# Unread products ahead of early TensorE steps: their number taken from a replay of all engines and of TensorE's instruction supply

## The chip, the cores and the metric

The kernel runs on one core of a Trainium2 chip. Its engines are TensorE (PE in the profile, its weight loads PEld), VectorE (DVE), ScalarE (ACT), GpSimd (POOL) and SyncE (SP), which here issues nearly all transfers. The metric is the device time of one execution in microseconds (us), lower is better.

## The reference

```python
def attention(q, k, v):                    # B=8, H=8, S=576, D=64
    q_d, k_d, v_d = (a.reshape(8, 8, 144, 4, 64).mean(axis=3) for a in (q, k, v))
    out_up = np.repeat(sm_attn(q_d, k_d, v_d), 4, axis=2)     # softmax attention on means of four
    mask = np.abs(pos[:, None] - pos[None, :]) < 4            # and a local band of width 7
    scores = np.where(mask, q @ k.T / 8, -1e9)
    return out_up + softmax(scores) @ v
def ffn(x, w_in, w_out):                   # x: 4608 x 512, w_in: 512 x 2048, w_out: 2048 x 512
    h = x @ w_in
    return (h * np.cos(h)) @ w_out
```

The attention's output, 4608 tokens by 512, is the FFN's x.

## The kernel before

The attention is cut into 32 units, one for a batch and a pair of heads. The FFN works on twelve tiles of 384 tokens and sixteen chunks of 128 of the 2048 inner columns; its products are made of two f16 halves of each operand, three matmuls for one. The weights come as 64-bit words in two halves each (`wdi`, `wdo`) and are split on ACT, DVE and POOL while the first units run.

The units of batches 0 and 1 (NEARLY = 2) are the early part. Each has four steps on TensorE: local scores in `u_s` (two mask products of 128 x 192 at L1022, then 192 small products of 32 x 32 at L1028), pooled scores in `u_s` (four of 72 x 144, L1037), transposes in `u_t` (eight of 72 x 72, L1153), and in `u_pv` the pooled PV (32 of 64 x 144, L1179) and the local PV (96 small ones of 64 x 24, L1196). Between them DVE, ACT and POOL make the softmax: for the first unit the local weights are `sml`, which DVE transposes at L1136 ahead of L1196; the pooled queries and keys of the next unit (`qkd`, L721) come from a chain on DVE. The result of L1196 is copied by ACT (L651, tile `xd`) and added by DVE (L1215). Later units run in pieces (L755 to L858). `gemm1` (L1410) is the first FFN product, `gemm2` (L1430) the second, and L1335 squares weights and inputs for a bound.

The order on all engines is written by a planner (class `Plan`). It holds every operation with a cost, a list scheduler (`run`) places them, and the kernel issues them in order of the planned start times `o.start`, each engine in that order. The planner also counts TensorE's instructions (L305 to L313): with FETCH it supposes that TensorE runs out of instructions after 448, and gets 256 more at a time; the wait is `o.stall`, which is part of `o.dur`.

The loop that issues the operations (L1608 to L1640) puts unread products ahead of PE operations that are planned to start before 300 us (`fend`). Such a product, `wide(s)`, multiplies the 128 x 128 identity `ident_b` with a 128 x 512 copy of itself (L1600) into a PSUM bank that is free for the moment, and nobody reads it. It reads no new data, so it never waits for a transfer. Two rules set their number. The first fills planned gaps: between the end of the last PE operation and the planned start it takes the planned ends of the helpers' operations in between as marks, and puts 0.8 (`fill`) times the gap over 0.22 us there; the first product behind a mark waits for that helper. The second adds products while the planned busy share of PE's recent past, `share(o, t)`, is under a bound, 0.42 (`share`) or, for some us after a stall of over 1 us, 0.72 (`again`). Both count in planned times; `cur` is where PE would stand with the products put in so far.

```python
n = int((y - x) * CFG["fill"] / 0.22)
...
while 4.0 < o.start < CFG["watch"] and share(o, max(cur, o.start)) < (CFG["again"] if cur < risk else CFG["share"]):
```

## Time and profile before

| what | us |
|---|---|
| runs of the kernel, median of 3 (lowest to highest) | 912.93 (911.85 to 913.46) |
| the profiled execution, first to last instruction | 910.3 |
| TensorE busy, matmuls | 889.4 |
| DVE busy | 711.2 |
| ACT busy | 693.1 |
| POOL busy | 486.2 |
| chain that ended last, part of L1600 (unread products) | 3% |

The profile is of another execution than the three runs; its span stands 2.6 us below their median. An engine's busy time adds up its instructions; an unread product counts like any other. "issue" in a list of waits is time in which the engine waited for nothing that the profile shows. [...] In windows the columns "busy (x)" hold us and the number of instructions.

### The profile page before, as it was taken

To read this page: it belongs to the slowest core of one execution; us is meant where nothing else is said; L and a number is where in the kernel's file an instruction comes from. 1 tells how busy PE (TensorE), PEld (TensorE's weight loads), DVE (VectorE), ACT (ScalarE), POOL (GpSimd) and SP (SyncE) were. 2 spreads that over 40 slices of the span, in tenths; PEclk is the share of its full clock that TensorE was granted. 3 is DMA by queue.
4 is the path that set the end of the run, shared out by engine and by line. 5 is a ranking of instruction groups with operands and counts; after the bars stand their busy time and mean duration, and the time that the engine had idled before them with its cause. 6 is when DMAs were issued, how large, how long until landed. Compare 5 with 4: busy or idle time off the path is not lost.

```text
span 910.3 us, 28740 instructions
## 1 busy us (share of the span) xinstructions
PE 889.4 (98%) x11673; PEld 579.9 (64%) x11673; DVE 711.2 (78%) x1514; ACT 693.1 (76%) x1542; POOL 486.2 (53%) x601
## 2 busy tenths in 40 slices
PE   8999999999999999999999999999999999999996
PEld 4665665555555555677767677666776777777773
DVE  6479788888889998877689887986689867846772
ACT  3458898888678876886887886986888987776764
POOL 4288753537768875644356543653468734522221
PEclk9899999999999999999999999999999999999998
DMA  7864176205453743232433443344344431124501
GB/s 245 255 223 142 37 276 214 83 1 95 113 131 80 169 99 99 63 94 67 119 88 101 121 114 96 89 111 125 102 135 119 112 105 38 56 96 140 174 2 39
DMA packets 100863, 103.96 MB, mean 114 GB/s; under 512 B 47280, under 2 KB 73648, under 8 KB 100720
## 3 DMA queue, kind: packets, MB, share of 16 engines
q1 hardware_dynamic: 99424, 99.67, 37.5%
q0 software_dynamic: 1296, 2.36, 1.8%
q8 instruction: 93, 1.52, 0.7%
q14 instruction: 50, 0.41, 0.1%
HBM read 81.05 MB, written 16.22 MB: 107 GB/s over the span
## 4 chain that ended last, share of the span: by engine, by line
PE 83%; DVE 7%; ACT 5%; DMA 2%; issue 2%; POOL 1%; SPq 0%; DVEq 0%; POOLq 0%; ACTq 0%
PE bank L1430 36%; PE bank L1335 22%; PE bank L1410 11%; PE bank L1600 3%; PE bank L906 2%; PE bank L1203 1%; PE bank L1184 1%; PE bank L912 1%; DMA q<-qT 1%; PE bank L1179 1%; DVE prob L932 1%; PE bank L1196 1%; PE bank L858 1%; ACT L946 1%; ACT L1389 1%
## 5 line engine op out<-in xcount | busy, mean ns | idle before, releaser
L1335 PEld LDWEIGHTS <-wdi 128*128 128x128 f16 x2400 | 203.8, 98 | 59.7 <-issue 3.8
L1430 PE MATMUL bank<-wdo,gh 128*128 128x512 f16 x696 | 207.1, 379 | 0.0
L1335 PE MATMUL bank<-wdo,wdi 128*128 128x192 f16 x1344 | 141.7, 246 | 0.8 <-DVE wdi L1356 0.3
L1430 PE MATMUL bank<-wdo,gl 128*128 128x512 f16 x348 | 131.7, 379 | 0.0
L1410 PEld LDWEIGHTS <-wdi 128*128 128x128 f16 x768 | 74.3, 98 | 56.3 <-issue 2.4
L530 POOL TENSOR_TENSOR gl<-tr,gh 128x384 f16<-128x384 f32 x60 | 59.2, 987 | 69.3 <-ACT gh L1393 51.0
L1430 PEld LDWEIGHTS <-gh 128*128 128x128 f16 x696 | 63.9, 98 | 41.4 <-issue 1.5
L1430 PE MATMUL bank<-wdo,wdi 128*128 128x512 f16 x342 | 86.9, 379 | 0.5 <-ACT ob L1448 0.5
L1430 PE MATMUL bank<-wdo,wdo 128*128 128x512 f16 x315 | 79.8, 379 | 0.7 <-ACT ob L1448 0.7
L1389 ACT ACTIVATE tr<-tr 128x384 f32<-128x384 f32 x98 | 50.9, 521 | 20.8 <-DVE tr L1387 20.3
L1430 PEld LDWEIGHTS <-gl 128*128 128x128 f16 x348 | 34.0, 98 | 41.1
L1386 ACT ACTIVATE tr<-bank,bmagic 128x384 f32<-128x384 f32 x66 | 37.8, 573 | 19.0 <-PE bank L1410 9.9
L1390 ACT ACTIVATE tr<-tr 128x384 f32<-128x384 f32 x98 | 50.4, 517 | 1.2
L1391 DVE SCALAR_TENSOR_TENSOR tr<-tr,bank 128x384 f32<-128x384 f32 x66 | 36.0, 545 | 18.0 <-ACT tr L1390 17.7
L1430 PEld LDWEIGHTS <-wdo 128*128 128x128 f16 x342 | 32.1, 98 | 28.1 <-issue 1.7
L1430 PEld LDWEIGHTS <-wdi 128*128 128x128 f16 x342 | 32.2, 98 | 27.2 <-issue 1.5
L530 POOL TENSOR_TENSOR gl<-wdo,gh 128x384 f16<-128x384 f32 x28 | 26.2, 937 | 43.3 <-ACT gh L1393 31.5
L1251 DVE TENSOR_TENSOR rec<-rec 128x192 f32<-128x192 f32 (+2 forms) x92 | 47.0, 512 | 0.7
L1351 DVE TENSOR_TENSOR bank<-bank,wdo 128x384 f32<-128x384 f32 x64 | 35.9, 560 | 14.6 <-PE bank L1335 13.8
L956 POOL TENSOR_TENSOR prob<-prob,su 128x432 f32<-128x432 f32 x24 | 24.4, 1018 | 37.9 <-DVE su L953 28.7
L530 POOL TENSOR_TENSOR wdo<-rec,wdo 128x384 f16<-128x384 f32 (+1 forms) x36 | 34.1, 953 | 17.2 <-ACT wdo L1296 11.2
L530 POOL TENSOR_TENSOR gl<-wdi,gh 128x384 f16<-128x384 f32 x28 | 28.3, 1010 | 26.6 <-ACT gh L1393 25.6
(408 smaller groups left out, 2451.8 us busy)
## 6 DMA issues: line engine op xcount, KB each, us to landing
vl<-vl SPq DMA_DIRECT2D x26, 384.0 KB, 3.8
vd<-vdn SPq DMA_DIRECT2D x24, 384.0 KB, 3.9
wdi<-w_in SPq DMA_DIRECT2D x16, 512.0 KB, 6.0
wdo<-w_out SPq DMA_DIRECT2D x16, 512.0 KB, 7.4
again<-w_in SPq DMA_DIRECT2D x32, 256.0 KB, 3.4
again<-w_out SPq DMA_DIRECT2D x32, 256.0 KB, 3.6
q<-qT SPq DMA_DIRECT2D x26, 292.0 KB, 4.0
k<-kT SPq DMA_DIRECT2D x26, 292.0 KB, 3.9
```

Of the source, the lines that this page charges most:

```text
L530: f = lambda e: lambda: e.tensor_tensor(out=out(), in0=in0(), in1=in1(), op=ALU.subtract)
L956: f = lambda e, get=get, by=by: lambda: e.tensor_tensor(out=get(), in0=get(), in1=by(), op=ALU.mult)
L1251: f = lambda e: lambda: e.tensor_tensor(out=out(), in0=in0(), in1=in1(), op=op)
L1335: pe.matmul(bank.get()[:, half * HT:(half + 1) * HT], w(i, a), x(l, a), start=start and k == 0, stop=k == 5, skip_group_check=not start)
L1351: pl.op("DVE", _dve(TT), lambda: dve.tensor_tensor(out=by.get()[:, :TT], in0=by.get()[:, :TT], in1=s.get(), op=ALU.add), r=[mid, s], w=[by])
L1386: pl.op("ACT", _act(m, banked, 1), lambda: act.activation(tr.get(), h(), AF.Identity, bias=bmagic), r=r, w=[tr])
L1389: pl.op("ACT", _act(m, False), lambda: act.activation(tr.get(), tr.get(), AF.Sin, scale=PI / fm.h), w=[tr], tab="sin")
L1390: pl.op("ACT", _act(m, False), lambda: act.activation(tr.get(), tr.get(), AF.Square, scale=math.sqrt(fm.ratio)), w=[tr])
L1391: pl.op("DVE", _dve(m), lambda: dve.scalar_tensor_tensor(out=tr.get(), in0=tr.get(), scalar=0.5 * fm.ratio, in1=h(), op0=ALU.subtract, op1 ...
L1410: pe.matmul(ph.get()[:, :m], w[:, i, kc, :], x[:, kc, :], start=(n == 0), stop=(n == 3 * KC - 1))
L1430: pe.matmul(o, (gh, gh, gl)[k].get()[:, sl], wo.get()[:, (0, 1, 0)[k]], start=(c == c0 and k == 0), stop=(c == c1 - 1 and k == 2))
L1600: return pe.matmul(s[2].get(), ident_b, ident_b.unsqueeze(1).broadcast_to([P, 4, P]), start=True, stop=True)
```

## The change

The planner keeps its numbers under the name PLANNED, and the order of all real operations stays as it is. The issuing loop carries a `Replay` along: it gives every operation of every engine a begin and an end from the ends of what it depends on and from its engine's last end, with the planner's latencies, and it counts TensorE's instructions one by one, unread products included: 448 are there at first, every 256 a further supply is asked for, which is there 2.5 us later. An unread product takes 0.22 us, and twice that before 4.6 us (WARM). The gaps that are filled are those of the replay, and so is the busy share; a product goes in only while it ends before the point to which the gap is to be filled. The bound of the second rule is 0.42 everywhere; `again`, `risk`, `cool` and `least` are used no more.

```diff
@@ -59,7 +59,8 @@
 THIRD = 20
 SLACK = 1.0
 
-FETCH = (448, 10.6, 256, 17.0, 5.2, 3.6)
+FETCH, WARM = (448, 256, 2.5), 4.6
+PLANNED = (448, 10.6, 256, 17.0, 5.2, 3.6)
...
@@ -238,7 +239,7 @@
                     heapq.heappush(soon[e], (0.0, i, o))
         locked = False
         cur, pen, tol, queue = None, CFG["tabpen"], CFG["alttol"], CFG["queue"]
-        issued, edge, there = CFG["lead0"], FETCH[0], FETCH[1]
+        issued, edge, there = CFG["lead0"], PLANNED[0], PLANNED[1]
         start, n = {}, 0
         while n < len(self.ops):
             best = None
@@ -307,8 +308,8 @@
                     part = max(0, edge - issued) / max(1, o.num)
                     o.stall = max(0.0, there - (t + part * dur))
                     there = max(there, t + part * dur)
-                    there += FETCH[4] if there < FETCH[3] else FETCH[5]
-                    edge += FETCH[2]
+                    there += PLANNED[4] if there < PLANNED[3] else PLANNED[5]
+                    edge += PLANNED[2]
                     dur += o.stall
                 issued += o.num
             start[o] = (t, e, dur, o.stall)
@@ -357,8 +358,56 @@
         for o in self.ops:
             o.start, o.eng, o.dur, o.stall = start[o]
             o.fn = o.alts[o.eng][1]
-            o.end = o.start + o.dur
+            o.end, o.base = o.start + o.dur, o.alts[o.eng][0]
         return sorted(self.ops, key=lambda o: (o.start, o.i))
+
+
+class Replay:
+
+    def __init__(self, engines):
+        self.free, self.end, self.spent = {e: {"SP": 1.6, "PE": CFG["f0"]}.get(e, 0.0) for e in engines}, {}, []
+        self.used, self.edge, self.limit, self.asked = 0, FETCH[1], FETCH[0], []
+
+    def begin(self, o):
+        def late(d):
+            if d.eng == o.eng:
+                return 0.0 if o.eng == "PE" else CFG["latself"]
+            return CFG["latpe"] if o.eng == "PE" else CFG["lat"] if d.eng == "PE" else CFG["late"]
+        return max([self.free[o.eng]] + [self.end[d] if g is None else self.end[d] + g + late(d) for d, g in o.preds])
+
+    def burst(self, t, dur, n):
+        if not n:
+            return t + dur
+        step, left = dur / n, n
+        while left:
+            k = min(left, self.edge - self.used, self.limit - self.used)
+            t, self.used, left = t + k * step, self.used + k, left - k
+            if self.used == self.edge:
+                self.asked.append(t + FETCH[2])
+                self.edge += FETCH[1]
+            if self.used == self.limit and left:
+                t, self.limit = max(t, self.asked.pop(0)), self.limit + FETCH[1]
+        return t
+
+    def filler(self, x):
+        t = max(self.free["PE"], x)
+        self.free["PE"] = self.burst(t, 0.22 * (2.0 if t < WARM else 1.0), 2)
+        self.spent.append((t, self.free["PE"], 1.0))
+
+    def share(self, o, t):
+        e = t + o.base
...
+
+    def put(self, o, t):
+        if o.eng == "PE":
+            e = self.burst(t, o.base * (2.0 if t < WARM else 1.0), o.num)
+            self.spent.append((e - o.base, e, o.util))
+        else:
+            e = t + o.dur
+        self.end[o] = self.free[o.eng] = e
+
+
 def _mmr(n, k, small):
     return k * (n / 2400.0 + 0.0027) if small else k * n * 0.0004543
 
@@ -1593,50 +1642,42 @@
         return sorted(out, key=lambda d: d.end)
 
     made, spent = {}, []
-    last = cur = CFG["f0"]
-    risk = 0.0
+    last = CFG["f0"]
 
     def wide(s):
         return pe.matmul(s[2].get(), ident_b, ident_b.unsqueeze(1).broadcast_to([P, 4, P]), start=True, stop=True)
 
-    def share(o, t):
-        e = t + o.dur - o.stall
...
+    replay = Replay(pl.engines)
 
     final = max(i for i, o in enumerate(order) if o.eng == "PE")
     with tc.manual_schedule():
         constants()
         for i, o in enumerate(order):
+            begin = replay.begin(o)
             if o.eng == "PE" and o.start < CFG["fend"]:
 
                 ahead = o.name in ("u_s", "u_t", "u_pv") and o.arg[0] == 0
                 s = (last, 0.0, idle) if ahead else spare(last, o.start)
                 if s:
-                    marks = [(s[0], None)]
+                    marks = [(replay.free["PE"], None)]
                     for d in before(o, s[0]):
-                        if d.end - marks[-1][0] > 0.4 and o.start - d.end > 0.4:
-                            marks.append((d.end, d))
-                    least = CFG["warm"] if ahead else 0
-                    for (x, d), (y, _) in zip(marks, marks[1:] + [(o.start - 0.2, None)]):
-                        n = int((y - x) * CFG["fill"] / 0.22)
-                        if y > o.start - 0.3:
-                            n = max(n, least)
-                        for j in range(n):
+                        e = replay.end[d]
+                        if e - marks[-1][0] > 0.4 and begin - e > 0.4:
+                            marks.append((e, d))
+                    for (x, d), (y, _) in zip(marks, marks[1:] + [(begin - 0.2, None)]):
+                        j, stop = 0, x + (y - x) * CFG["fill"]
+                        while max(replay.free["PE"], x) + 0.22 < stop:
                             ins = wide(s)
-                            spent.append((max(cur, x), max(cur, x) + 0.22, 1.0))
-                            cur = max(cur, x) + 0.22
-                            if d and not j:
+                            replay.filler(x)
+                            j += 1
+                            if d and j == 1:
                                 tc.add_manual_dep(ins.ins, made[d].ins.name, mybir.DependencyInfo(
                                     mybir.DependencyClass.Sync, mybir.DependencyReason.DATA), reason="spread")
-                    while 4.0 < o.start < CFG["watch"] and share(o, max(cur, o.start)) < (CFG["again"] if cur < risk else CFG["share"]):
+                    while 4.0 < o.start < CFG["watch"] and replay.share(o, max(begin, replay.free["PE"])) < CFG["share"]:
                         wide(s)
-                        spent.append((cur, cur + 0.22, 1.0))
-                        cur += 0.22
-                if o.stall > 1.0:
-                    risk = max(cur, o.start) + o.stall + CFG["cool"]
+                        replay.filler(0.0)
                 last = o.start + o.dur
-                cur = max(cur, o.start) + o.dur
-                spent.append((cur - o.dur + o.stall, cur, o.util))
+            replay.put(o, max(begin, replay.free[o.eng]))
             made[o] = o.fn()
             if small and i == final:
                 outside = nc.values_load(flag[0:1, 0:1], min_val=0, max_val=1,
```

On DVE, ACT, POOL and SP no instruction moves, and TensorE's real instructions keep their order. What changes is the number of unread products, 135 before and 109 now, in TensorE's stream of 23,465 instructions. The lines in the kernel's body stand 49 further down in the changed file (L1196 is L1245), and `wide` goes from L1600 to L1648. From the start, ahead of:

| step | before | now |
|---|---|---|
| first L1022 | 19 | 10 |
| first L1037 | 3 | 4 |
| second L1037 | 10 | 0 |
| third L1022 | 9 | 10 |
| third L1037 | 0 | 4 |
| second L1153 | 3 | 0 |
| fourth L1022 | 0 | 3 |
| first L1179 | 1 | 1 |
| first L1196 | 18 | 3 |
| all from there to the first L1410 | 28 | 28 |
| all behind it | 44 | 46 |

(Each step counts runs of its line: the "second L1037" is the pooled score step of the second unit.)

TensorE, at the pooled scores of the second unit. Before (`mask` and `ident_b` are constants, `wxo`, `wxi` and `qkd` hold queries and keys; ten pairs of L1600 stand there):

```order
L1022 MATMUL bank<-mask,ident_b 128x192
L1028 MATMUL bank<-wxo_153,wxi_149 32x32 x48
L1600 LDWEIGHTS ident_b
L1600 MATMUL bank<-ident_b 128x512
...
L1600 LDWEIGHTS ident_b
L1600 MATMUL bank<-ident_b 128x512
L1037 MATMUL bank<-wxi_149 72x144 x4
```

Now:

```order
L1071 LDWEIGHTS ident_b
L1071 MATMUL bank<-mask,ident_b 128x192
L1077 MATMUL bank<-wxo_153,wxi_149 32x32 x48
L1086 MATMUL bank<-wxi_149 72x144 x4
L1648 LDWEIGHTS ident_b
L1648 MATMUL bank<-ident_b 128x512
```

Ten pairs went; the pooled scores follow the local ones at once, and ten stand behind them where nine stood.

TensorE, from the pooled PV to the local PV of the first unit. Before (`vd` and `vl` are the values, `ptd` and `sml` the pooled and the local weights; 18 pairs of L1600 stand ahead of L1196):

```order
L1600 MATMUL bank<-ident_b 128x512
L1179 MATMUL bank<-ptd,vd_309 64x144 x16
L1600 LDWEIGHTS ident_b
L1600 MATMUL bank<-ident_b 128x512
...
L1600 LDWEIGHTS ident_b
L1600 MATMUL bank<-ident_b 128x512
L1196 MATMUL bank<-sml,vl 64x24 x48
L1153 MATMUL bank<-wxi_149 72x72 x4
```

Now:

```order
L1648 MATMUL bank<-ident_b 128x512
L1228 MATMUL bank<-ptd,vd_301 64x144 x16
L1648 LDWEIGHTS ident_b
L1648 MATMUL bank<-ident_b 128x512
L1648 LDWEIGHTS ident_b
L1648 MATMUL bank<-ident_b 128x512
L1648 LDWEIGHTS ident_b
L1648 MATMUL bank<-ident_b 128x512
L1245 MATMUL bank<-sml,vl 64x24 x48
L1202 MATMUL bank<-wxi_149 72x72 x4
```

Fifteen of the 18 pairs went; the real steps on both sides are the same.

## Rows read from the trace of the kernel before

**Rows 1.** The page: span and busy time of each engine.
```profile
span 910.3 us, 28740 instructions
...
PE 889.4 (98%) x11673; PEld 579.9 (64%) x11673; DVE 711.2 (78%) x1514; ACT 693.1 (76%) x1542; POOL 486.2 (53%) x601
```

**Rows 2.** Busy time by stretch; columns stand in the first line.
```profile
core 0: us, PE busy (x) PEld busy (x) DVE busy (x) ACT busy (x) POOL busy (x), PEclk, DMA share, GB/s
28.10:35.40 7.30, 7.30 (x115) 3.56 (x113) 0.00 (x0) 0.00 (x0) 0.37 (x1) 0.74 0.84 273
36.10:60.00 23.90, 23.90 (x544) 17.49 (x542) 16.79 (x43) 13.77 (x46) 15.96 (x24) 1.00 0.65 192
66.00:88.00 22.00, 21.14 (x277) 11.09 (x275) 20.00 (x40) 19.60 (x44) 19.20 (x25) 1.00 0.51 160
...
300.00:600.00 300.00, 294.96 (x4068) 199.24 (x4067) 247.56 (x529) 238.15 (x531) 169.25 (x198) 1.00 0.38 100
```

**Rows 3.** Waits of PE, 0 to 60 us: us in total, times, longest.
```profile
PE bank L1600 <- issue: 1.6, 1, 1.6
PE bank L1600 <- POOL ident_b masks.py:199: 1.3, 1, 1.3
PE bank L1028 <- issue: 1.2, 1, 1.2
PE bank L1153 <- DVE qkd L721: 0.3, 1, 0.3
```

**Rows 4.** Chain that ended last, 0 to 45 us: start, us, what.
```profile
1.34 5.85 PE bank L1600 x19
...
10.95 1.19 issue
...
12.39 2.27 PE bank L1600 x10
...
22.51 1.61 issue
...
24.51 3.50 PE bank L1179 x32
28.01 5.91 PE bank L1600 x18
...
41.01 2.11 PE bank L1179 x32
```

**Rows 5.** Instructions of tile `sml`, 0 to 40 us: ns min/median/max, first and last start.
```profile
L1196 PE MATMUL bank<-sml,vl x96: 211/211/232, 33.9 to 35.2; 32*64 32x24 f32 x96
...
L1136 DVE STREAM_TRANSPOSE sml<-sml x1: 564/564/564, 20.6 to 20.6; 128x384 f32<-128x384 f32 x1
```

**Rows 6.** Timeline of DVE, 35 to 37 us: start, us, what, idle time before.
```profile
35.81 0.82 DVE L1215 TENSOR_TENSOR smd<-bank,xd 128x288 f32<-128x288 f32 x2 [8.08 <-ACT xd L651]
```

**Rows 7.** Busy time by stretch, from the start; columns as in Rows 2.
```profile
0.00:9.90 9.90, 8.56 (x130) 4.05 (x130) 3.81 (x10) 1.28 (x1) 6.99 (x33) 1.00 0.76 244
0.00:11.50 11.50, 9.61 (x222) 4.96 (x223) 5.41 (x15) 1.28 (x1) 7.25 (x33) 1.00 0.76 237
0.00:21.40 21.40, 18.53 (x380) 10.33 (x380) 12.76 (x36) 5.80 (x23) 8.72 (x36) 1.00 0.79 244
0.00:23.50 23.50, 19.64 (x476) 11.27 (x476) 14.50 (x40) 7.66 (x28) 10.04 (x39) 1.00 0.78 245
```

**Rows 8.** The page: DMA queue, kind: packets, MB, share of 16 engines.
```profile
q8 instruction: 93, 1.52, 0.7%
```

**Rows 9.** L1600 alone by stretch: PE and PEld busy, PEclk, DMA share, GB/s.
```profile
28.00:31.80 3.80, 3.80 (x10) 1.32 (x11) 0.50 0.89 295
31.80:33.90 2.10, 2.10 (x10) 0.80 (x8) 0.98 0.73 206
```

**Rows 10.** Timeline of POOL, 4.9 to 5.4 us.
```profile
5.15 0.10 POOL L452 MEMSET mask<- 32x5 bf16 x1
```

**Rows 11.** Waits of SP's queue, 0 to 60 us; columns as in Rows 3.
```profile
SPq L684 <- PE bank L1179: 8.1, 2, 6.4
```

More of the change, by code (lines that the diff above doesn't have):

```diff
@@ L128 @@
     __slots__ = ("eng", "dur", "fn", "tab", "deps", "sdeps", "now", "start", "end", "lat", "name", "arg", "preds", "succs",
-                 "i", "fin", "bank", "alts", "boost", "shares", "util", "slack", "lead", "num", "stall")
+                 "i", "fin", "bank", "alts", "boost", "shares", "util", "slack", "lead", "num", "stall", "base")
 class Plan:
@@ L359, in schedule @@
             o.fn = o.alts[o.eng][1]
-            o.end = o.start + o.dur
+            o.end, o.base = o.start + o.dur, o.alts[o.eng][0]
         return sorted(self.ops, key=lambda o: (o.start, o.i))
+class Replay:
[27 more added lines that the diff above has]
+        e = t + o.base
+        return (sum(max(0.0, min(y, e) - max(x, e - 3.41)) * u for x, y, u in self.spent[-60:]) + o.base * o.util) / 3.41
+    def put(self, o, t):
[5 more added lines that the diff above has]
+        self.end[o] = self.free[o.eng] = e
 def _mmr(n, k, small):
@@ L1595, in attn_ffn_kernel @@
     made, spent = {}, []
-    last = cur = CFG["f0"]
-    risk = 0.0
+    last = CFG["f0"]
     def wide(s):
         return pe.matmul(s[2].get(), ident_b, ident_b.unsqueeze(1).broadcast_to([P, 4, P]), start=True, stop=True)
-    def share(o, t):
-        e = t + o.dur - o.stall
-        return (sum(max(0.0, min(y, e) - max(x, e - 3.41)) * u for x, y, u in spent[-60:]) + (o.dur - o.stall) * o.util) / 3.41
+    replay = Replay(pl.engines)
     final = max(i for i, o in enumerate(order) if o.eng == "PE")
```

## Prediction

> **What bounds the kernel now.** I read the page's busy shares first, then busy time by stretch, then TensorE's waits in the first 60 us, the chain of waits there, and single tiles. TensorE (PE) is busy 98% of a span of 910.3 us [rows 1]. From 300 to 600 us it works 294.96 of 300 us, with DVE and ACT near 80% [rows 2]: that part starts when the early part lets it and then takes its own time. The change touches only unread products before 300 us, so the question is how early TensorE gets through its real early work. Being busy says little there, because an unread product counts as busy. Four waits of PE are all that the first 60 us have, none for a transfer: two of 1.2 and 1.6 us on "issue", in which PE waited for nothing that the profile shows, 0.3 us for DVE's `qkd`, and the start [rows 3]. The rest of the delay is work put in the way. The chain shows it: 19 unread products take 5.85 us at the start, 10 take 2.27 us, and 18 take 5.91 us from 28.01 us [rows 4]. Behind those 18 stands the first local PV step (L1196). Its last input, the transposed `sml`, starts at 20.6 us and takes 0.56, so it is there at 21.2 us; the step starts at 33.9 us [rows 5]. DVE stands idle 8.08 us until the step's result has been copied [rows 6], and from 28.1 to 35.4 us DVE and ACT do nothing at all [rows 2]. So at this place unread products, not inputs, set the pace.
>
> **The two "issue" waits.** PE instructions (matmuls plus weight loads) up to 9.9, 11.5, 21.4 and 23.5 us are 260, 445, 760 and 952 [rows 7], and the waits stand at 10.95 and 22.51 us [rows 4]. A queue of kind "instruction" moves 1.52 MB in 93 transfers, about 16 KB each [rows 8]; at 65 bytes an instruction (an estimate: 1.52 MB over the 23,346 of PE and PEld [rows 1]) that is some 250 each. My reading: PE begins with about 448 instructions, asks for 256 more near the 256th and again near the 768th, gets them some 2.3 and 2.7 us later (12.14 - 9.9 and 24.1 - 21.4), and runs dry near 448 and 960 if it gets there first. Two unread products are four instructions, so removing them also moves where it runs dry. [...]
>
> **The change, place by place.** The order of the real operations on all engines is unchanged; only the number of unread products differs: 135 before, 109 after. I follow how far ahead of its old place PE is. One such product costs 2.10/10 = 0.21 us at the granted clock of 0.98, and 3.80/10 = 0.38 us at 0.50 [rows 9].
> 1. Before the first mask product 19 become 10. The 19 take 5.85 us [rows 4], the first ones more than the last; those taken away are the last: 9 x 0.21 = 1.9 us. PE is then through at about 5.3 us, and the mask's last piece is written at 5.15 + 0.10 us [rows 10], so no wait follows. Ahead 1.9.
> 2. First L1037: 3 become 4, -0.2. Ahead 1.7.
> 3. Second L1037: 10 become 0, 2.27 us [rows 4], though these also carried PE past instruction 448. Eight products fewer stand before the 256th instruction, so it is today's 272nd, in the second L1028 near 10.1 us, and comes at 10.1 - 1.7 = 8.4; the answer is there at about 10.75, and PE stands at 448 near 9.5: a wait of about 1.25 us, as long as today's 1.19. Ahead 3.9.
> 4. Third L1022 9 become 10, third L1037 0 become 4: -1.1. Ahead 2.8.
> 5. The 0.3 us for `qkd` [rows 3] goes, since DVE's chain, which hangs on the second L1037, starts about 4 us sooner. What is late next is L1153 on the same chain, and it has more room than it had. Ahead 3.1. Three products move from the second L1153 to the fourth L1022: 0.
> 6. Second supply wait: 13 products fewer stand before the 768th instruction, so it is today's 794th, near 21.5 us, and comes at 18.4; the answer is there at 21.1. Instruction 960 is 12 products into L1179, near 20.3: 0.8 us instead of 1.61. Ahead 3.9.
> 7. First pooled PV step (L1179): 3.50 us today at a reduced clock, 2.11 us when it runs again [rows 4]; I credit 1.4. Ahead 5.3.
> 8. First L1196: 18 become 3, 5.91 - 3 x 0.21 = 5.3 us. Ahead 10.6. A third supply wait may now show: 0 to 0.3, taken 0.1. Ahead 10.5 at 36 us.
> 9. From there to the first FFN product 28 stand where 28 stood. TensorE is busy 23.90 of 23.90 us from 36.1 to 60, DVE 16.79 and ACT 13.77 [rows 2], so they can follow an earlier PE, and SP's `vdn` loads that wait for L1179 (8.1 us in two waits [rows 11]) leave sooner too. Behind the first L1410 there are 46 for 44: 0.
>
> No wait is added to a real operation: the unread products that wait wait for helpers that the next real step needs anyway, so that costs nothing at the least and, if a replayed time is off, under 0.3 us each.
>
> Against the 10.5 I set two bounded terms. **Helpers**: from 66 to 88 us DVE works 20.0, ACT 19.6 and POOL 19.2 of 22 us [rows 2], so this stretch cannot be compressed; its start moves up only if the work before it fits into the 7.3 us in which DVE and ACT now idle. Between 0 (all fits) and 2 us (a quarter of the idle time is of no use) I take 1.2. [...] A dip over ten products costs 10 x 0.17 plus some small ones, 2.2 us; no dip costs 0. I take 1.3, since the stretch now has fewer wide products. Gain 10.5 - 1.2 - 1.3 = 8.0 us: a span of 902.3. The profiled execution's span is 2.6 us under the median of the runs, 912.93 us, so the forecast on that scale is 912.9 - 8.0 = **905.0 us**.
>
> **The rivals.**
> - *Slower: the clock stays low.* What the rows show: after the wait of 1.61 us and the light L1179 (3.50 us) the clock was 0.50, and it was 0.98 only after the 18 unread products had run for some 4 us [rows 4, 9]. Exactly these become 3. If the clock falls at the first supply wait, near 11 us, and stays down until the wide FFN products come near 55 us, 49 unread products cost 0.17 more each (8.3), four L1179 1.4 more each (5.6), and the small products between 0 and 5.6, say 3: 16.9 us against a gain of 10.5 - 1.2 = 9.3, so 7.6 slower, **920.5 us**. It decides where low clock fills more than 9.3/16.9 of those 44 us, about 24 us. Against it: behind L1196 the counts are as today, where the clock is 1.00 throughout [rows 2]. [...] Chance 0.11.
> - *Smaller gain.* The clock falls after the second supply wait, as today, and recovers some 20 us later, since the 18 are gone. Then L1179 keeps its 3.50 us (the 1.4 is lost), the next L1179 costs 1.4 more, and 13 unread products 0.17 each (2.2), small ones 0.5: 5.5 of the 8.0 + 1.3 go, **909.1 us**. Chance 0.17.
> - *Absorbed.* The weights and the helpers, not PE, set the start of the stretch from 66 us, and the 10.5 us turn into a PE that waits for DVE and ACT: **912 us**, no change. For it: 20.0 of 22 us on DVE. Against it: from 28.1 to 35.4 us DVE waits for PE. Chance 0.06.
> - That the change doesn't do what it says is excluded for the counts, which stand in the order; that PE runs dry elsewhere than its replay thinks is in the terms 3, 6 and 8, some 2 us in all.
>
> **How the numbers follow.** The forecast has 0.66: gains of 5.5 to 11.5 us, 901.5 to 907.5, from the terms' bounds. With the smaller gain that is 0.83 for faster; absorbed 0.06 for the same; 0.11 for slower. A measurement of this kernel tells 0.2%, about 1.8 us, from no change. The range goes from 901.5, the forecast's best end, to 911.5, which takes in the smaller gain and the edge of the absorbed case and leaves out the slower rival and the tails.
>
> **What would show it.** In the chain of the changed kernel L1600 ahead of the first L1196 falls from x18 to x3, and L1196 starts near 23.5 us instead of 33.9; the first "issue" wait stands near 9.5 us with 1.2 to 1.4 us, the second near 20 us and under 1 us; L1179 takes about 2.1 us at clock 1.00; DVE's idle 8.08 us before L1215 shrinks to under 2. From 300 us on every stretch's sum is as before, 8 us sooner. The forecast is wrong if the granted clock is 0.50 for over 10 us between 10 and 60 us, if PE gains new waits for DVE or ACT between 60 and 90 us that add up to the lead, or if supply waits grow beyond 3.5 us together.

## The result and the profile after

The changed kernel is slower: a median of 916.48 us in 20 runs (912.38 to 924.99), against 911.89 us for the kernel before in 20 runs of its own (906.97 to 915.72). The ratio is 1.0062, with a 95% interval of 1.0039 to 1.0086. The forecast was 905.0 us, faster.

The page of the changed kernel, span and busy time, against [rows 1]:

```profile
span 914.7 us, 28686 instructions
...
PE 885.2 (97%) x11647; PEld 576.9 (63%) x11647; DVE 710.9 (78%) x1514; ACT 692.6 (76%) x1542; POOL 485.5 (53%) x601
```

TensorE has 52 instructions fewer and works 4.2 us less, DVE, ACT and POOL work what they did, and the span is 4.4 us longer: TensorE stands still 8.6 us longer than before (29.5 us of its span, against 20.9).

The early part first. The chain of the changed kernel that ended last, 0 to 30 us (start, us, what), against [rows 4]; L1228, L1245 and L1648 are L1179, L1196 and L1600 of the kernel before:

```profile
1.34 3.98 PE bank L1648 x10
...
9.78 0.69 issue
...
16.25 0.83 issue
...
20.27 0.88 PE bank L1228 x11
21.15 1.79 issue
22.94 1.51 PE bank L1228 x21
24.45 0.75 PE bank L1648 x3
25.20 1.52 PE bank L1245 x96
```

The 18 unread products are three, and L1245 starts at 25.2 us instead of 33.9. There are three supply waits where there were two. In DVE's timeline the idle 8.08 us of [rows 6] are 0.78:

```profile
27.08 0.82 DVE L1264 TENSOR_TENSOR smd<-bank,xd 128x288 f32<-128x288 f32 x2 [0.78 <-ACT xd L700]
```

So the early part did what it should. To see what became of it I took each real TensorE instruction (the unread ones left out, both traces have the same 11,538 matmuls in the same order) and subtracted its start in the changed kernel from its start in the kernel before. Positive is sooner; the times on top are those of the kernel before.

| us in the kernel before | 36 | 60 | 125 | 135 | 145 | 260 | 270 | 310 | 600 | 800 |
|---|---|---|---|---|---|---|---|---|---|---|
| lead of the changed kernel, us | 8.7 | 7.9 | 7.5 | 6.4 | 2.1 | 2.1 | -2.9 | -4.3 | -4.1 | -4.2 |

Both sides are single executions, of 910.3 and 914.7 us. The lead is 7.5 us at 125 us. It is lost at three places, near 130, 265 and 300 us (5.4, 5.0 and 2.6 us); between 270 and 290 us 1.2 us come back, and elsewhere it hardly moves. TensorE's waits on "issue" from 120 to 310 us (us in total, times, longest), in the changed kernel:

```profile
PE bank L961 <- issue: 5.0, 2, 2.8
PE bank L1459 <- issue: 4.0, 2, 3.1
```

and in the kernel before:

```profile
PE bank L906 <- issue: 0.3, 1, 0.3
```

Four waits of 9.0 us together, for nothing that the profile shows: the same kind as the waits at 10.95 and 22.51 us of [rows 4], ten times further into the program. The timeline of TensorE in the changed kernel at two of them:

```profile
129.88 0.52 PE L961 MATMUL bank<-qkd 64*32 64x144 f32 x15
133.16 0.48 PE L961 MATMUL bank<-qkd 64*32 64x144 f32 x15 [2.76 <-issue]
...
262.69 0.49 PE L1459 MATMUL bank<-x2h,wdi 128*128 128x384 f16 x2
266.29 0.34 PE L1459 MATMUL bank<-x2l,wdi 128*128 128x384 f16 x1 [3.11 <-issue]
```

Both stop in the middle of a step, between two products of the same group, where the profile shows nothing to wait for. How many instructions had TensorE run by then? Busy time of the changed kernel from the start to four such places (columns as in [rows 2]):

```profile
0.00:125.90 125.90, 119.20 (x2255) 74.33 (x2256) 95.34 (x229) 87.82 (x221) 81.54 (x137) 1.00 0.66 203
0.00:132.90 132.90, 123.39 (x2382) 76.76 (x2383) 100.86 (x236) 92.30 (x229) 87.82 (x142) 1.00 0.68 213
0.00:266.00 266.00, 253.10 (x3656) 146.54 (x3656) 212.65 (x441) 194.10 (x428) 160.09 (x227) 0.99 0.53 155
0.00:302.40 302.40, 287.20 (x4163) 165.35 (x4163) 241.88 (x502) 221.53 (x482) 185.04 (x261) 0.99 0.51 148
```

PE and PEld make 4511, 4765, 7312 and 8326. These columns leave out semaphore instructions; with the 33, 35, 48 and 58 of them in TensorE's records up to there, the stops stand exactly at 4544, 4800, 7360 and 8384, which is 448 + 256 x 16, 17, 27 and 31. TensorE ran out of instructions. The wait isn't all. Busy time around these places:

```profile
core 0: us, PE busy (x) PEld busy (x) DVE busy (x) ACT busy (x) POOL busy (x), PEclk, DMA share, GB/s
126.00:130.00 4.00, 3.79 (x119) 2.22 (x126) 3.77 (x6) 3.08 (x7) 3.83 (x5) 1.00 1.05 380
130.00:134.00 4.00, 1.24 (x43) 0.70 (x30) 1.65 (x3) 1.29 (x3) 2.35 (x2) 1.00 1.07 372
134.00:138.00 4.00, 4.00 (x15) 1.73 (x13) 0.55 (x2) 0.99 (x2) 0.10 (x1) 0.57 0.42 155
264.00:268.00 4.00, 1.71 (x9) 0.95 (x10) 2.51 (x8) 0.09 (x1) 1.79 (x3) 0.94 0.64 196
268.00:272.00 4.00, 4.00 (x14) 1.65 (x13) 2.71 (x7) 3.84 (x7) 2.34 (x5) 0.63 0.17 29
300.00:304.00 4.00, 1.77 (x34) 0.80 (x14) 3.56 (x10) 3.24 (x5) 2.33 (x5) 1.00 1.05 276
```

PEclk is the granted clock, as a share of TensorE's full one and a mean of the stretch; the records of both traces hold 1.00 and 0.50 alone, and within the first 900 us 0.50 stands from 25.1 to 31.8 us before, and from 134.5 to 137.8 and 267.6 to 270.9 us now. Behind the waits of 2.76 and 3.11 us it is 0.57 and 0.63 in 4 us, although TensorE is busy all of the time again: the wide products that follow run slowly for some 3 us. Behind the wait of 2.23 us near 300 us it stays at 1.00. That makes the loss near 130 us 5.4 us (7.5 to 2.1), more than its two waits of 0.9 and 2.76.

### The profile page after: what moved, and what is told of

It is laid out like the page before. It is cut to its first block, busy times and chain, and to the rows that moved or that the text cites. A ratio compares the mean times of both kernels' runs of the same rounds, so it can differ in the third digit from the quotient of the medians.

```text
span 914.7 us, 28686 instructions
## 1 busy us (share of the span) xinstructions
PE 885.2 (97%) x11647; PEld 576.9 (63%) x11647; DVE 710.9 (78%) x1514; ACT 692.6 (76%) x1542; POOL 485.5 (53%) x601
## 4 chain that ended last, share of the span: by engine, by line
PE 84%; DVE 7%; issue 3%; ACT 2%; DMA 2%; POOL 1%; SPq 1%; DVEq 0%; POOLq 0%; ACTq 0%
PE bank L1479 36%; PE bank L1384 21%; PE bank L1459 13%; PE bank L955 2%; PE bank L1648 2%; PE bank L1252 2%; PE bank L1233 2%; DMA q<-qT 1%; PE bank L961 1%; PE bank L1228 1%; PE bank L1245 1%; PE bank L907 1%; DMA vl<-vl 1%; DVE prob L981 1%; PE bank L1202 1%
## 5 line engine op out<-in xcount | busy, mean ns | idle before, releaser
L1459 PEld LDWEIGHTS <-wdi 128*128 128x128 f16 x768 | 74.4, 98 | 60.7 <-issue 7.6
L1435 ACT ACTIVATE tr<-bank,bmagic 128x384 f32<-128x384 f32 x66 | 37.8, 573 | 26.8 <-PE bank L1459 17.5
L1440 DVE SCALAR_TENSOR_TENSOR tr<-tr,bank 128x384 f32<-128x384 f32 x66 | 36.1, 546 | 18.9 <-ACT tr L1439 18.7
L1436 DVE SCALAR_TENSOR_TENSOR tr<-tr,bank 128x384 f32<-128x384 f32 x66 | 37.4, 567 | 11.3 <-ACT tr L1435 10.9
```

The lines of the kernel that those rows point to most:

```text
L1435: pl.op("ACT", _act(m, banked, 1), lambda: act.activation(tr.get(), h(), AF.Identity, bias=bmagic), r=r, w=[tr])
L1436: pl.op("DVE", _dve(m), lambda: dve.scalar_tensor_tensor(out=tr.get(), in0=tr.get(), scalar=MAGIC * fm.h, in1=h(), op0=ALU.subtract, op1=A ...
L1440: pl.op("DVE", _dve(m), lambda: dve.scalar_tensor_tensor(out=tr.get(), in0=tr.get(), scalar=0.5 * fm.ratio, in1=h(), op0=ALU.subtract, op1 ...
L1459: pe.matmul(ph.get()[:, :m], w[:, i, kc, :], x[:, kc, :], start=(n == 0), stop=(n == 3 * KC - 1))
```

## The experiments

**The theories.** A: from some place on, all that matters is TensorE's instruction count there. Instructions come in pieces of 256, the spacing of the stops above; a piece arrives some time after it was asked for, and if TensorE runs through the instructions in between faster than that, it stands still. The change takes 52 instructions out of the early part, so every later edge of 256 falls on other instructions, among them bursts of light ones. B: the count is innocent, and the later stretches, which start 7.5 us sooner, meet other transfers. Both are told apart by instructions that do next to nothing: products of the 32 x 32 corner of an identity, in fp32, four instructions each, into the spare bank.

**e1: the count restored.** The changed kernel, with `pads = 13` set ahead of the loop:

```diff
+                if s and pads and o.start > 60.0:
+                    for _ in range(pads):
+                        pe.matmul(s[2].get()[:32, :32], ident[:32, :32], ident[:32, :32], start=True, stop=True)
+                    pads = 0
                 last = o.start + o.dur
```

> The changed kernel with 13 tiny fp32 products of 32x32 (52 TensorE instructions) ahead of a step planned near 60 us, so that from there on TensorE's instruction count is again that of the kernel before. Theory A (the count decides where TensorE runs dry later): the waits of 1.2, 3.0, 3.4 and 2.5 us near 125, 130, 263 and 300 us go, the lead of 7.5 us that stands at 120 us is kept, 904 to 906 us, ratio to the kernel before 0.991 to 0.994. Theory B (the early work comes 7.5 us sooner and its later stretches fall under other transfers): the waits stay, 915 to 917 us, ratio 1.003 to 1.006.

907.47 us, ratio 0.9953 (0.992 to 0.9987). Faster than the kernel before, 9 us faster than the changed one, through 52 instructions that compute nothing. B's 915 to 917 us is not what came. It isn't the 904 to 906 that A expected either. The profiled execution, 915.26 us, is the second longest of the twelve, so its trace shows what stood against the gain there and not the usual run. Its four longest supply waits past 60 us are 0.4 to 0.7 us each, 2.0 together, but the clock fell in the early part:

```profile
24.00:36.00 12.00, 12.00 (x189) 0.57 0.75 234
36.00:60.00 24.00, 24.00 (x544) 1.00 0.82 242
```

(PE busy, PEclk, DMA share, GB/s.) Its lead goes from 7.2 us at 30 us to 3.8 at 60, where the changed kernel's profile, with a clock of 1.00 there, kept 7.9. Past 60 us it loses 6.9 us more, half of it near 273 us:

```profile
PE bank L1459 <- DVE tr L1440: 2.5, 1, 2.5
...
PE bank L955 <- issue: 0.7, 1, 0.7
```

That is no supply wait. DVE is 2.5 us late with `tr`, and the granted clock from 130 to 300 us is 0.99 on the mean; the kernel before waits 1.0 us there, e4 2.8 and e12 2.9. In e12 the chain that ends with `tr` leads back to a transfer of `q` that took 7.8 us. So a late transfer, of the kind that B has in mind, costs something too, but at another place: the changed kernel waits 0.4 us for this `tr`. What speaks against B is the time of the twelve runs, then e2, and the trace of e9, which is 9.6 us ahead at 125 us without such waits.

**e2: the count of the changed kernel, in the kernel before.** The same lines with `pads = 51` in the kernel before: 204 more is 52 fewer, in pieces of 256.

> The kernel before, all its unread products kept, with 51 tiny fp32 products of 32x32 (204 instructions) ahead of a step planned near 60 us; 204 more is 52 fewer, counted in pieces of 256. Theory A: the waits of the changed kernel appear near 133, 137, 265 and 300 us, some 10 us together with the clock that falls behind them, plus 1 to 3 us for the tiny products: 921 to 925 us, ratio 1.009 to 1.015. Theory B: nothing but the tiny products, 912 to 915 us, ratio 1.000 to 1.003.

924.88 us, ratio 1.0147 (1.0097 to 1.0197), as A expected. TensorE's waits from 120 to 330 us:

```profile
PE bank L912 <- issue: 4.5, 2, 2.9
PE bank L1410 <- issue: 4.3, 2, 4.1
```

The same two steps as in the changed kernel (L912 and L1410 are L961 and L1459 there), though not one instruction of the early part was touched. The stops stand one piece further on, at 5056, 7616 and 8640 instructions. The tiny products were dearer than the 1 to 3 us of the expectation: the lead falls by 4.8 us over them (-0.9 to -5.7).

**e3: another count.** The changed kernel with `pads = 36`.

> The changed kernel with 36 tiny products (144 instructions), a count at which, going by the starts in the trace of the kernel before, the fewest edges of 256 fall into runs of light instructions. Theory A: late waits of 0 to 3 us in all, 902 to 907 us, ratio 0.989 to 0.995, and at other places than in either kernel. Theory B: waits as in the changed kernel, 916 to 919 us, ratio 1.004 to 1.008.

906.07 us, ratio 0.9937 (0.9908 to 0.9965): A. Past 60 us there is no supply wait over 0.2 us by the list of waits. The 36 products, 9.8 to 6.0 us of lead, cost 3.8 us, of which they take some 2.4 themselves; the rest goes with the clock, which fell right behind the light block, as it did in e2 (PE busy, PEclk, DMA share, GB/s):

```profile
60.00:66.00 6.00, 6.00 (x106) 1.00 0.96 332
66.00:72.00 6.00, 6.00 (x85) 0.72 1.07 369
```

**e4: one place alone.** The kernel before, with only three of the 18 unread products ahead of the first L1196, and `pads = 8`:

```diff
+                npv, put = npv + (o.name == "u_pv"), 0
...
                         for j in range(n):
+                            put += 1
+                            if o.name == "u_pv" and npv == 2 and put > 3:
+                                cur = max(cur, x) + 0.22
+                                spent.append((cur - 0.22, cur, 1.0))
+                                continue
                             ins = wide(s)
...
-                        wide(s)
+                        put += 1
+                        if o.name != "u_pv" or npv != 2 or put <= 3:
+                            wide(s)
```

> The kernel before with 3 instead of 18 unread products ahead of the first L1196 alone, and 8 tiny products (32 instructions) near 60 us in place of the 30 that went. The prediction's step 8 alone: up to 5.3 us sooner at 36 us, less up to 2 where the clock stays low longer, and under theory A kept to the end: 906 to 909 us, ratio 0.993 to 0.997. If a single place gives nothing because the next waits take it: 911 to 913 us.

908.14 us, ratio 0.9958 (0.9924 to 0.9993), as expected. Its lead is 6.9 us at 36 us, already without any other place of the change, and 6.0 at 260. That is more than the 5.3 us of the place itself: its second supply wait was 0.8 us for 1.61, and its clock stayed at 1.00 where the profile of the kernel before has 0.50 [rows 9].

**How far ahead.** The records of the 93 instruction transfers fit best if a piece is asked for some 100 instructions before TensorE executes the multiple of 256 (from 770 to 901 us in the kernel before they start 73 to 99 ahead of it), so some 300 before the place where it runs dry. With that, a count can be judged ahead of a run: from the trace of the kernel before, take the time that the 300 instructions before each edge need, and add up what is missing to an answer of 4.5 or 6.5 us. Two counts test this, the best and the worst by that sum, with the tiny products put singly ahead of steps, `pads = 26` (e5) and `pads = 3` (e6):

```diff
-                    for _ in range(pads):
+                    for _ in range(min(pads, 1)):
...
-                    pads = 0
+                    pads -= min(pads, 1)
```

> The changed kernel with 26 tiny products (104 instructions) singly ahead of 26 steps from 60 us on. Theory A, now with numbers: the traces so far put the request for each 256 some 300 instructions ahead of the place where TensorE runs dry, so what counts is how long the 300 instructions before that place take. By their times in the trace of the kernel before, this count has the smallest sum of shortfalls of all (0.2 us for an answer of 4.5 us, 11 for one of 6.5; the changed kernel's own 1.1 and 23): waits after 60 us under 1 us in all, 903 to 905.5 us, ratio 0.989 to 0.993. Rival (any count but the changed kernel's is about as good): 906 to 908, as with 13 or 36 tiny products.

> The changed kernel with only 3 tiny products (12 instructions) from 60 us on: by the same sum the worst count of all (2.4 and 28 us). Theory A: at least as slow as the changed kernel, 917 to 922 us, ratio 1.005 to 1.012. Rival: the waits hang on something else that these 12 instructions also upset, 905 to 912 us.

e6 gave 917.54 us, ratio 1.0092 (1.0057 to 1.0126), inside its range; past 60 us it waits

```profile
PE bank L961 <- issue: 8.5, 3, 4.4
...
PE bank L1459 <- issue: 1.1, 1, 1.1
```

9.6 us for instructions, at the same four counts as the changed kernel with its 9.0. That it is worse than the changed kernel isn't shown: the intervals overlap (1.0039 to 1.0086 there). e5 was a miss in time: 908.17 us, ratio 0.9989 (0.9962 to 1.0016). Its count did what was said: of TensorE's waits past 60 us none is on "issue". But the 26 products cost 5.1 us (lead 0.8 at 60 us, -4.3 at 110), 0.2 us each: put singly, a tiny product takes as long as a wide unread one. Its early lead was small as well, 5.0 us at 30 us behind a wait of 3.16 us at instruction 960, and its clock was 0.54 from 24 to 39 us. So the traces bear out which counts wait; the times don't, for e5's is that of its rival (906 to 908), and e3 has no late supply wait either. By the traces the carrier was wrong, not the count.

**e7: almost no unread products.** The changed kernel without the 11th to the 86th:

```diff
-                            ins = wide(s)
+                            wides += 1
+                            kept = not 10 < wides <= 86
+                            ins = wide(s) if kept else None
```

> The changed kernel without the 11th to the 86th of its unread products (10 at the start and the last 23 stay); 152 fewer instructions is, in pieces of 256, the same count as with 26 tiny products. It tells what the unread products between 5 and 60 us are worth for the clock. If the clock stays at 1.00 without them: 53 x 0.21 = 11 us less on TensorE before 60 us, of which waits for helpers leave 3 to 6: 898 to 902 us, ratio 0.984 to 0.989. If it falls to 0.50 for 20 us or more (the slower rival of the prediction): 908 to 916 us, ratio 0.996 to 1.005.

913.92 us, ratio 1.0035 (1.0007 to 1.0062). Busy time by stretch:

```profile
0.00:12.00 12.00, 8.75 (x262) 5.01 (x264) 7.43 (x20) 3.34 (x11) 7.24 (x33) 1.00 0.74 228
12.00:36.00 24.00, 22.61 (x482) 20.46 (x467) 15.90 (x41) 11.74 (x42) 8.32 (x14) 0.50 0.82 246
36.00:63.00 27.00, 26.37 (x388) 21.06 (x386) 15.26 (x36) 9.36 (x30) 14.54 (x22) 0.50 0.75 230
```

Without them TensorE's granted clock stays at 0.50 from 12 to 63 us, when the wide FFN products come. The lead is 10.5 us at 30 us, 0.8 at 60 and -2.6 from 90 us on. This is the mechanism of the prediction's slower rival, at its full length. In the changed kernel, which keeps these products, it doesn't happen at that length: the mean granted clock of e7's twelve runs is 0.960 to 0.972, that of the changed kernel's 20 runs 0.979 to 0.995.

**e8: one place and the best count.** The kernel of e4 with 20 tiny products put singly.

> The kernel before with 3 instead of 18 unread products ahead of the first L1196 and 20 tiny products from 60 us on, which gives the best count. If this one place and the count carry the whole gain: within 1.5 us of the changed kernel with 26 tiny products, 904 to 906.5 us, ratio 0.990 to 0.994. If the other places of the change carry 2 us or more: 906.5 to 909.

907.8 us, ratio 0.9982 (0.9954 to 1.0011). It is within 0.4 us of e5, as the first alternative says, and in the time range of the second. Its count is two instructions short of e5's (80 for the 30 that went). Neither is told from the kernel before; what they show is that the other places of the change bring no gain beside this one that can be seen. They are 2.7 and 1.3 us over what was expected, by the price of the tiny products (here a lead of 6.9 at 70 us and 3.1 at 110).

**e9 to e12: the count for nothing.** An unread product of 128 x 512 can be split into two of 128 x 256: the same columns, two instructions more. `wide` counts its calls and splits the later ones, past the 57th in e9:

```diff
+    halved = [0]
     def wide(s):
+        halved[0] += 1
+        if halved[0] > 57:
+            return [pe.matmul(s[2].get()[:, n:n + 256], ident_b, ident_b.unsqueeze(1).broadcast_to([P, 2, P]), start=True, stop=True)
+                    for n in (0, 256)][0]
         return pe.matmul(s[2].get(), ident_b, ident_b.unsqueeze(1).broadcast_to([P, 4, P]), start=True, stop=True)
```

e12 splits past the 83rd (52 instructions, the count of the kernel before). e10 is e4's one place without tiny products, split past the 79th. e11 splits past the 69th and puts six more ahead of the first L1245, so 9 instead of 3:

```diff
+                npv += o.name == "u_pv"
+                if o.name == "u_pv" and npv == 2:
+                    for _ in range(6):
+                        wide(s)
                 last = o.start + o.dur
```

> The changed kernel with its last 52 unread products each split into two of 128x256: the same columns and the same time by the number of columns, but 104 instructions more, the count that had no wait over 0.35 us behind 60 us with 26 tiny products. Theory A: the early lead (8.7 us at 36 us in the changed kernel) stays to the end where the clock holds: 903 to 905 us; where the clock falls to 0.50 near 24 us, as in two of five profiles of kernels with this early part, 907 to 910. Median 904 to 907, ratio 0.989 to 0.995. Rival (a half product costs as much as a whole one): 5 to 10 us more, 910 to 916.

> The kernel before with 3 instead of 18 unread products ahead of the first L1196, and its last 41 unread products split into halves (82 instructions for the 30 that went: the same count for the late part). The lead of this one place was 6.9 us at 36 us in two profiles, with the clock at 1.00. Theory A: kept to the end, 904 to 906 us, ratio 0.990 to 0.994, and less spread than the kernels with the whole early change.

> The changed kernel with 9 instead of 3 unread products ahead of the first L1245 and the last 46 halved. It tells whether these products hold the clock there. If they do: 1.3 us later at 36 us than with 3, but no execution with the clock at 0.50 near 24 to 36 us: 904 to 907 us with a spread under 6 us. If the fall comes earlier, from the waits for instructions at 17 to 23 us: the same spread as with 3, median 1.3 us later.

> The changed kernel with its last 26 unread products halved: 52 instructions, so the count of the kernel before from there on, now without the price of tiny products. Theory A: the late waits are those of the kernel before (0.5 to 0.8 us each, some 2 us in all): 1 to 2 us later than with 52 halved, 904 to 908 us, ratio 0.991 to 0.996.

| kernel | median us (lowest to highest) | ratio (95%) |
|---|---|---|
| e9, whole change, 104 more | 903.02 (899.96 to 905.78) | 0.9905 (0.9882 to 0.9928) |
| e10, one place, the same count | 902.68 (901.86 to 907.57) | 0.9909 (0.9885 to 0.9933) |
| e11, whole change, 9 ahead, the same count | 902.46 (900.8 to 903.85) | 0.9894 (0.9876 to 0.9912) |
| e12, whole change, 52 more | 904.62 (902.62 to 912.26) | 0.9917 (0.9898 to 0.9937) |

All four beat both kernels. e9, e10 and e11 came in 1.0 to 1.5 us under their ranges; only e12 lies inside. e12 and e9 overlap, so the times don't show that e9's count is better than that of the kernel before. e10's spread, 5.7 us, is no smaller than e9's, against what was expected. e10 stands with e9 and e11 within the intervals, so at the same count the other places of the change bring nothing that these runs can tell from the one ahead of the first L1196. Leads against the kernel before, worked out as above:

| us in the kernel before | 36 | 60 | 125 | 145 | 260 | 310 | 600 | 800 |
|---|---|---|---|---|---|---|---|---|
| changed kernel | 8.7 | 7.9 | 7.5 | 2.1 | 2.1 | -4.3 | -4.1 | -4.2 |
| e2, count of the changed kernel | -0.9 | -0.9 | -5.8 | -10.6 | -10.6 | -17.5 | -16.7 | -16.8 |
| e7, almost no unread products | 9.7 | 0.8 | -2.6 | -2.8 | -2.7 | -1.6 | -0.6 | -0.8 |
| e9, 104 more by halves | 9.6 | 9.6 | 9.6 | 9.9 | 9.9 | 11.0 | 12.4 | 12.1 |
| e12, 52 more by halves | 5.6 | 4.4 | 4.4 | 4.1 | 4.1 | 2.0 | 0.8 | 0.0 |

These are single executions, and not all are usual ones: e2's is 4.3 us over its median, e12's 7.6 over, e9's 2.9 under. How far an early lead moves from one execution to the next is seen at the one place of e4 and e10: 6.9 us at 36 us in e4, 3.5 in e10, which had waited 3.2 us at instruction 448.

In e9 the halves cost nothing (9.6 us at 60 and at 125 us), and nothing is lost behind. It gains 2.5 us more: the kernel before has 1.0 us of small supply waits past 60 us, and waits 1.0 us for `tr` near 273 us. Its waits past 60 us are led by those that every kernel here has, and "issue" isn't among them:

```profile
PE bank L1384 <- POOL wdo L579: 1.6, 1, 1.6
PE bank L1384 <- DVE wdi L1440: 1.3, 1, 1.3
```

The profiled execution of e12 is one of those whose clock fell early. PE busy, PEclk, DMA share and GB/s of 25 to 36 us in e9:

```profile
25.00:36.00 11.00, 11.00 (x261) 1.00 0.85 266
```

in e11:

```profile
25.00:36.00 11.00, 11.00 (x248) 0.89 0.77 242
```

and in e12:

```profile
25.00:36.00 11.00, 11.00 (x218) 0.59 0.77 247
```

Near 24 us it fell in the profiles of e1, e5 and e12, and not in those of the changed kernel, e3, e6 and e9, all with three products ahead of L1245. With nine (e11) it fell shortly, and the six runs lie within 3.1 us of each other, against 5.8 in e9 and 9.6 in e12. Whether the six more wide products made the difference isn't shown, with one profile each.

## Why the prediction was wrong

**Right, place by place.** Step 1 said 1.9 us ahead, the trace has 1.9. Step 3 said 3.9; it was 4.4, since the first supply wait was 0.69 us and not 1.25. Step 5's 0.3 us wait for `qkd` is gone. Step 7 credited 1.4; the 32 products took 2.4 us for 3.50, so 1.1. Step 8, 18 to 3, gave 5.91 - 0.75 = 5.2 for 5.3. Step 6 was mis-sized: the second wait is 1.79 us, not 0.8, and a third of 0.83 us stands between the two (I had put it later, at 0.1). So L1245 led by 8.7 us, not 10.5. The clock's term, a fall of the granted clock from 1.00 to the 0.50 of [rows 9] over ten products, was 1.3, which no run shows: it was 0 in the profile of the changed kernel and 3.4 in e1's. The helpers' term was 1.2 us, and from 36 to 90 us the lead falls by 1.2, but that is luck: TensorE's waits for DVE and ACT in this stretch are 0.9 us in both traces, and 0.8 of the 1.2 go at two more edges, 0.4 each at instructions 1472 and 2240. Together 8.0 were forecast behind 90 us and 7.5 were there, with the 1.8 too much in the steps and the 1.3 too much for the clock nearly cancelling.

**Where it failed.** Step 9 and the sentence behind it: "Behind the first L1410 there are 46 for 44: 0", on the ground that the later part "starts when the early part lets it and then takes its own time". It doesn't take its own time: it takes one that depends on the instruction count with which it is entered. The prediction itself said that removing two instructions "also moves where it runs dry", and then followed this for 24 us instead of to the end. The term it left out is the supply waits past 60 us: 9.0 us of waits and some 4 us lost with them, most of it to the clock behind two of them, in the changed kernel, against 0.3 from 120 to 310 us before. e1 and e9 take the term away by the count alone, e2 puts it into the kernel before, e6 keeps it with 12 instructions more. Of its conditions for being wrong the last, supply waits "beyond 3.5 us together", is what happened, but I had thought of the early ones.

**The rivals.** The slower one had the sign and not the mechanism: in the profiled execution of the changed kernel the granted clock from 12 to 75 us was 1.00 (PE busy, PEclk, DMA share, GB/s):

```profile
12.00:75.00 63.00, 59.65 (x1206) 1.00 0.86 259
```

Five of its 20 runs took over 920.5 us, with a mean granted clock of 0.979 to 0.986 against 0.993 in the profiled one; where it fell in them no profile shows. e7 shows that the rival's price was real, 13 us from the lead at 30 us to that at 90, waits for helpers included, if those products go: the granted clock is 0.50 there from 12 to 63 us. The smaller gain exists too: the leads of e1, e5 and e12 fell by 3.4 to 4.2 us between 30 and 60 us where the clock had fallen near 24 us, and those of other profiles with the same early part did not: it depends on the execution. Absorption by helpers played no part: the lead is 7.9 us at 60 us and still 7.5 at 90.

**The instruction supply.** The prediction's reading, some 448 instructions at the start and 256 more at a time, is borne out: TensorE's stops stand at 448 + 256 x n, and 93 transfers of kind "instruction" lie within the span of either kernel. What the edges cost is not one number: 9.0 us of waits in one kernel and 0.3 in the other from 120 to 310 us, and e1 against the changed kernel prices it at 9 us.

**Open.** What makes the answer to a request late wasn't tried. The records of the transfers narrow it down. Counted from the place 100 instructions ahead of each multiple of 256, a piece's transfer starts some 1.3 us later in the median of the changed kernel, and 4 to 7 us later for the four pieces behind the long waits. The transfer takes about 1 us, and TensorE goes on 1.5 us after it has landed. The 300 instructions ahead of these four places take 4.9 to 6.8 us. So they do at some 20 other places past 60 us (3.4 to 7.0 us), where TensorE stood still for 0.5 us at most, because the piece was there 0.8 to 3.7 us after the same place. A long wait needed both, then: quick instructions and a late answer. Which instructions fall ahead of an edge is the count's doing. The late answers stand where the kernel's own transfers are dense: a DMA share of 1.05 to 1.07 from 126 to 134 and 300 to 304 us, and 1.10 from 262 to 264 us. Whether the pieces queue behind those transfers isn't shown: no kernel here took them away.

## What to carry to other kernels

In a long unrolled stream like TensorE's here, with stops at 448 + 256 x n, an edit that adds or removes instructions puts other instructions ahead of every later edge. Before pricing such an edit, mark these edges in the trace and look at how long the 300 instructions ahead of each take. In the changed kernel they took 4.9 to 6.8 us ahead of the four long waits, which lay at a DMA share of 1.05 to 1.10; as short a time had no long wait at some 20 other places. The slowest 300, ahead of instruction 5312, took 27.6 us, and TensorE didn't stop there. If the place can be chosen, choose it with instructions that take no time, here by splitting unread products in two; measured, that was worth 13 us between two kernels with the same early part (916.5 and 903.0).

## What the runs showed of the hardware that was not expected

- TensorE stopped for instructions at counts of exactly 448 + 256 x n up to 19,648, for 0.2 to 4.4 us, and 52 instructions more or fewer ahead of an edge decided whether the stops past 60 us were long.
- Two waits of about 3 us for instructions were followed by 3.3 us at a granted clock of 0.50 (134.5 to 137.8 and 267.6 to 270.9 us), with TensorE fully busy. Not every such wait was: behind a wait of 3.22 us in e10 (11.9 to 15.1 us) the clock was 1.00.
- A fp32 product of 32 x 32 with four instructions took 0.2 us when it stood alone among other steps (e5) and about 0.07 in a block of 36 (2.4 us, e3); two half-width unread products cost what a whole one did.
- The first wait for instructions, at 448, had a different length in each execution: 0.69 us in the changed kernel's profile, 1.19 in that of the kernel before, under 0.3 in e1 and e9, and over 3 in e2 and e10.
